# An attention and GEGLU kernel on one core: batch 0 in a new order, and gate matmuls placed around the last turn of each batch

## The chip, the core and the metric

The kernel runs on one core of a Trainium2 chip. The core has a matrix engine (PE, with its own queue of weight loads, PEld), a vector engine (DVE), a scalar engine (ACT) and GpSimd (POOL). SyncE (SP) and POOL also issue DMAs. Each engine works through its own instructions in program order, and they wait for each other through semaphores. Matmuls write into PSUM, of which this kernel uses all eight banks.

The metric is the device time of one execution in microseconds, as the median of several runs. One further execution was profiled. All times of single instructions are from that one.

## What is computed

There are 8 batches of 8 heads with 576 tokens of 64 elements, and 16 "beacon" keys and values in front of each head's own. After a causal softmax attention, the heads are put side by side to 4608 rows of 512, and a GEGLU block follows:

```python
k_all = np.concatenate([beacon_k, k], axis=2)
v_all = np.concatenate([beacon_v, v], axis=2)
scores = scale * np.matmul(q, k_all.transpose(0, 1, 3, 2))
scores = np.where(causal, -1000000000.0, scores)      # beacon columns are never masked
a = softmax(scores)
x = np.matmul(a, v_all)           # -> 4608 x 512
g, val = x @ w_gate, x @ w_val    # 512 x 1536 each
out = (gelu(g) * val) @ w_out     # 1536 x 512
```

Inputs and output are float32 in HBM. The loads convert to bfloat16 on the way.

## The kernel before, in words

Nearly every instruction is held in the order in which the program writes it (`keep`). So the order of the calls in the main loop is the order on each engine. The names that matter:

- A batch has four **pairs** of heads (`m` = 0 to 3). `scores(b, m, c)` (L205) does one of four chunks of transposed scores into a `psum_s` buffer and then an exponential on ACT into `expT`. Chunks 0 and 2 are called `ab(m)`, chunks 1 and 3 `cd(m)`. `masks` (L226) sets the masked triangle of `expT` to zero: on POOL (L239) for every batch but 0, on DVE (L236) for batch 0. `attend` (L254) is 30 small matmuls of `expT` with the values and a column of ones, `normalize` (L278) divides by the sum on DVE into `y_sb`; both together are `av(m)`. `turn(b, m)` (L294) transposes `y_sb` on PE and copies it on DVE into `xT_sb`, the input of the GEGLU block.
- `gate_val(ci, fi)` (L305) does one of 12 slices of the hidden layer for a chunk of 512 rows: 4 matmuls with the gate weights and 4 with the value weights (one for each `kk`, the four blocks of 128 of the input, which are the four pairs), into one `psum_s` buffer `gv_ps`. Then a GELU on ACT into `ge_sb`, and a product on DVE (L325) into `hT_sb`. The product is the last reader of `gv_ps`.
- `out_mms(ci, u0, u1)` (L330) does steps of the last matmul. A chunk has 48 steps, in four tiles of 12. After each 12th step DVE copies the tile out (L349) and SP stores it. The first tile of a chunk sits in `psum_t`, the others in `psum_o`. In the main loop `o(n)` means n steps of the chunk of the batch before.
- PSUM: `psum_s` has two buffers of two banks (scores, `gv_ps`, and one `attend` of batch 0), `psum_x` one of two banks (`attend`, and the PE transposes `t_ps`), `psum_t` and `psum_o` one bank each.
- Queries and keys of batches 0 and 1 are loaded by `load_qk6` and transposed on PE (`transpose_pe`, L162, 24 small transposes and one for the beacon keys, then two DVE copies into `qkT`). From batch 2 on they are loaded by `load_qk` into `q_sb` and `k_sb` and transposed by DMAs issued on SP (`transpose_dma`, L192).
- All loads are issued on POOL, in one queue with POOL's masks. Each issue from the ninth on waits until the DMA eight issues earlier has landed.

After the loads are issued, batch 0 does its four pairs with nothing to put between them but five `warm` matmuls (L187) after two of them; then 12 slices of `gate_val`, of which slices 6 to 9 are each followed by a `transpose_pe` of batch 1. From slice 0 on, the loads of batch 2 are queued on POOL. Batches 1 to 7 then have an attention part, in which the `o` steps fill the gaps, and a gate part of 12 slices. The first slice (`kk_late`) does its `kk` = 3 matmuls last, since those need the last turn. A last chunk of 512 rows is left over at the end.

The attention part of batches 1 to 7, in the order of PE before the change:

```
o5 ab0 o7 cd0 o5
ab1 av0 o3 cd1 o4 turn0
ab2 av1 o3 cd2 o5 turn1
ab3 av2 o4 cd3 o6 turn2
av3 o6 turn3  gate_val 0 .. 11
```

Of the kernel before, what the change touches and what calls it, by code (L numbers as in the profile page):

```python
# [7 lines left out]
P = 128  # L8
B, H, S, NB, D = 8, 8, 576, 16, 64
SK = S + NB  # L10
# [43 lines left out]
def kernel(  # L54
# [26 lines left out]

    ident = const.tile([P, P], BF16, name="ident", tag="ident")
    nc.vector.memset(ident, 0.0)
    wg_sb = const.tile([P, K_CHUNKS, D_FF], BF16, name="wg_sb", tag="wg_sb")
    wv_sb = const.tile([P, K_CHUNKS, D_FF], BF16, name="wv_sb", tag="wv_sb")
    wo_sb = const.tile([P, F_TILES, D_MODEL], BF16, name="wo_sb", tag="wo_sb")
# [22 lines left out]
    def dma(out_ap, in_ap):  # L109
        keep(nc.gpsimd.dma_start(out=out_ap, in_=in_ap))  # L110

    qk6 = {}

    def load_qk6(b, h0, h1):
        if b not in qk6:
            qk6[b] = (
                hpool.tile([P, 2, H, 6 * D], BF16, name="qk6", tag="hT_sb"),
                npool.tile([NB, H, D], BF16, name="kb", tag="kb"),
            )
        for w, src in enumerate((q, k)):  # L120
            dma(
                qk6[b][0][0:96, w, h0:h1, :],
                src[b, h0:h1, :, :].rearrange("h (p r) d -> p h (r d)", r=6),
            )

    def load_kb(b):
        dma(qk6[b][1], beacon_k[b].rearrange("h t d -> t h d"))

    def load_keys(src, beacon, dst, b):
        dma(dst[0:NB, 0, :, :], beacon[b].rearrange("h t d -> t h d"))  # L130
# [13 lines left out]
    def load_v(b):  # L144
        load_keys(v, beacon_v, v_ring[b % NRING][:, :, :, 0:D], b)

    def load_gate_val(i):
        fs = slice(i * 512, (i + 1) * 512)
        for w, dst in ((moe_w_gate, wg_sb), (moe_w_val, wv_sb)):
            keep(nc.gpsimd.dma_start(out=dst[:, :, fs], in_=w[:, fs].rearrange("(kk p) f -> p kk f", p=P)))  # L150

# [7 lines left out]
        keep(nc.scalar.activation(out_ap, in_ap, func, **kw))  # L159


    def transpose_pe(b, m, pool, tag):  # L162
        t_ps = pool.tile([P, 2, 1024], BF16, name="t_ps", tag=tag)
        qk, kb = qk6[b]

        def tr(out_ap, in_ap):
            n = in_ap.shape[0]
            keep(nc.tensor.transpose(out_ap, in_ap, ident[0:n, 0:n]))  # L168

        for w in range(2):  # L170
            for r in range(6):
                for hi in range(2):
                    tr(
                        t_ps[64 * hi : 64 * hi + 64, w, r * 96 : (r + 1) * 96],
                        qk[0:96, w, 2 * m + hi, r * D : (r + 1) * D],
                    )
        tr(t_ps[:, 1, S:SK], kb[:, 2 * m : 2 * m + 2, :])
        keep(
            nc.vector.tensor_copy(  # L179
                qkT[:, m, :, NB:SK].rearrange("p w (t r) -> p w t r", r=6),  # L180
                t_ps[:, 0:2, 0:S].rearrange("p w (r t) -> p w t r", r=6),
            )
        )
        keep(nc.vector.tensor_copy(qkT[:, m, 1, 0:NB], t_ps[:, 1, S:SK]))


    def warm(b, m, n):  # L187
        w_ps = psum_o.tile([P, D_MODEL], FP32, name="w_ps", tag="o")
        for _ in range(n):
            mm(w_ps, ident, qkT[:, m, 1, 0:512], True, True)  # L190

    def transpose_dma(b):  # L192
        q_sb, k_sb = q_ring[b % NRING], k_ring[b % NRING]
# [29 lines left out]
        if b:  # L223
            masks(b, m, c)

    def masks(b, m, c):  # L226
        expT = exp_of[b * NPAIR + m]
        for t, s_lo, _, _ in CHUNKS[c]:
            if s_lo != S_LO[t]:
                continue  # L230
            n = DIAG[t]
            d = expT[0 : KROWS[t], :, EXP_OFF[t] : EXP_OFF[t] + n]
            if b == 0:
                w = tri[0 : KROWS[t], NB : NB + n] if t == 0 else tri[0 : KROWS[t], 0:n]
                w = w.rearrange("p (o n) -> p o n", o=1).to_broadcast([KROWS[t], 2, n])
                keep(nc.vector.tensor_tensor(out=d, in0=d, in1=w, op=ALU.min))  # L236
            else:
                keep(
                    nc.gpsimd.affine_select(  # L239
                        out=d,  # L240
                        in_=d,
                        pattern=[[0, 2], [1, n]],
                        compare_op=ALU.is_ge,
                        fill=0.0,
                        base=NB if t == 0 else 0,
                        channel_multiplier=-1,
                    )
                )
# [42 lines left out]
                )  # L291
            )

    def turn(b, m):  # L294
        y_sb = y_of.pop(b * NPAIR + m).rearrange("p (j e) d -> p j (e d)", e=2)
        y_ps = psum_t.tile([P, 1024], BF16, name="y_ps", tag="t")
        for j in (4, 3, 2, 1, 0):
            n = P if j else S_LO[1]
            keep(nc.tensor.transpose(y_ps[:, Q_LO[j] : Q_LO[j] + n], y_sb[0:n, j, :], ident[0:n, 0:n]))  # L299
        keep(nc.vector.tensor_copy(xT_sb[:, m, b * S : (b + 1) * S], y_ps[:, 0:S]))  # L300


    h_of, o_of = {}, {}

    def gate_val(ci, fi, kk_late=False):  # L305
        if fi == 0:
            h_of[ci] = hpool.tile([P, F_TILES, CH], BF16, name="hT_sb", tag="hT_sb")
        n0 = ci * CH
        gv_ps = psum_s.tile([P, 2, CH], FP32, name="gv_ps", tag="s")
        order = [(w, kk) for w in range(2) for kk in range(K_CHUNKS)]  # L310
        if kk_late:
            order.sort(key=lambda t: t[1] == K_CHUNKS - 1)
        for w, kk in order:
            mm(
                gv_ps[:, w, :],
                (wg_sb, wv_sb)[w][:, kk, fi * P : (fi + 1) * P],
                xT_sb[:, kk, n0 : n0 + CH],
                kk == 0,
                kk == K_CHUNKS - 1,
                skip_group_check=True,  # L320
            )
        ge_sb = fpool.tile([P, CH], BF16, name="ge_sb", tag="ge_sb")
        act(ge_sb, gv_ps[:, 0, :], ACT.Gelu)
        keep(
            nc.vector.tensor_tensor(  # L325
                out=h_of[ci][:, fi, :], in0=gv_ps[:, 1, :], in1=ge_sb, op=ALU.mult
            )
        )

    def out_mms(ci, u0, u1, wide=lambda ti: False):  # L330
        for u in range(u0, u1):
# [22 lines left out]
    def by_diagonal(tile_, op, fill):  # L354
# [3 lines left out]
            )  # L358
        )

    load_qk6(0, 0, 2)
    by_diagonal(ident, ALU.not_equal, 1.0)
    load_kb(0)
    load_qk6(0, 2, 4)
    load_qk6(0, 4, H)
    by_diagonal(tri, ALU.is_ge, 0.0)
    load_v(0)
    for i in range(3):
        load_gate_val(i)
    load_qk6(1, 0, H)  # L370
    load_kb(1)
    load_out_w()
    load_v(1)
    transpose_pe(0, 0, psum_s, "s")
    for b in range(B):
        u = [0]

        def o(n):
            if b:
                out_mms(b - 1, u[0], u[0] + n, lambda ti: ti == 0)  # L380
                u[0] += n

        def ab(m):
            for c in AB:
                scores(b, m, c)

        def cd(m):
            for c in CD:
                scores(b, m, c)

        def av(m, wide=False):
            attend(b, m, wide)
            normalize(b, m)

        keep(nc.scalar.preload_act_table_set(SET_EXP))  # L395
        if b == 0:
            for m in range(NPAIR):
                ab(m)
                if m == NPAIR - 1:
                    for mm_ in (0, 1, 2):  # L400
                        for c in AB + CD:
                            if mm_ == 2 or (mm_ == 1 and c in CD):
                                masks(0, mm_, c)
                    av(0)
                    for c in AB:
                        masks(0, m, c)
                else:
                    transpose_pe(0, m + 1, psum_x, "x")
                    if m == 2:
                        for mm_, cs in ((0, AB + CD), (1, AB)):  # L410
                            for c in cs:
                                masks(0, mm_, c)
                cd(m)
                if 1 <= m < NPAIR - 1:
                    warm(b, m, 5)
            for c in CD:
                masks(0, NPAIR - 1, c)
            av(1)
            av(2, wide=True)
            turn(b, 0)  # L420
            turn(b, 1)
            av(3)
            turn(b, 2)
            turn(b, 3)
        else:
            o(5)
            ab(0)
            o(7)
            cd(0)
            o(5)  # L430
            for m in range(1, NPAIR):
                ab(m)
                av(m - 1)
                o((3, 3, 4)[m - 1])
                cd(m)
                o((4, 5, 6)[m - 1])
                turn(b, m - 1)
            av(3)
            o(6)
            turn(b, 3)  # L440
        keep(nc.scalar.preload_act_table_set(SET_GELU))
        for fi in range(F_TILES):
            gate_val(b, fi, kk_late=fi == 0)
            if b == 0 and 6 <= fi < 10:
                transpose_pe(1, fi - 6, psum_x, "x")
            if fi == 0:
                if b + 2 < B:
                    load_qk(b + 2)
# [37 lines left out]
```

## Time and profile before

| what | us |
|---|---|
| median of 4 runs (397.33 to 398.18) | 397.81 |
| the profiled execution | 397.34 |
| its span, first to last instruction | 395.6 |
| start to the first gate matmul of batch 0 (31.38) | 31.4 |
| gate part of batch 0, with the transposes of batch 1, to the first `o` step of batch 1 (55.98) | 24.6 |
| one later batch, from its first `o` step to that of the next one | 42.0 |
| of which attention with `o` steps | 21.3 |
| of which gate part | 20.7 |
| from the end of batch 7's gate part to the end | about 45 |

The span is shorter than the time of its execution by 1.7 us. Columns of the timeline are: start, duration, engine, line, operation, output and input with their shapes, how many instructions were merged into the row, and in brackets how long the engine stood idle before it and what ended that wait. Matmuls overlap at their ends, so a row's duration is longer than the step to the next row; steps between starts are what the engine takes.

### The profile page before, as it was taken

The page shows a single profiled execution, that of the slowest core. Times are in us where ns is not written, and L with a number is a line of the kernel's source. Part 1 is how long each engine was busy: PE and PEld are TensorE (multiplying, and loading weights), DVE is VectorE, ACT ScalarE, POOL GpSimd, SP SyncE. Part 2 cuts the span into 40 slices and gives each one's busy share as a digit, 9 for nine tenths or more (in the row PEclk, how much of TensorE's full clock was granted, in tenths as well). Part 3 has the DMA queues.
Part 4 walks back from the last instruction along what each step waited for, and adds up shares of the span by engine and source line. Part 5 has one row for each costly group of instructions (what it writes and reads, how often), then busy time and mean ns, then how long its engine had stood idle before and what let it go on. Part 6 is the DMA issues. An engine that isn't in the chain of part 4 may idle for free.

```text
span 395.6 us, 7386 instructions
## 1 busy us (share of the span) xinstructions
PE 371.3 (94%) x3010; PEld 183.0 (46%) x3010; DVE 167.2 (42%) x345; ACT 188.1 (48%) x252; POOL 155.6 (39%) x277
## 2 busy tenths in 40 slices
PE   3868999999999999999999999999999999999996
PEld 1454445544554445543544455444544455444442
DVE  1484554543354434433444345433444344332332
ACT  2852248433862378236833584338623782332210
POOL 8723494780368224941486047703300240000000
PEclk9999999999999999999999999999999999999999
DMA  7999996699029951998099916991142011000012
GB/s 95 177 206 204 179 135 90 65 155 139 35 56 150 134 65 46 136 151 83 29 116 141 101 55 67 151 135 36 55 104 44 30 41 41 2 0 28 29 51 106
DMA packets 139153, 36.23 MB, mean 92 GB/s; under 512 B 126832, under 2 KB 134512, under 8 KB 139120
## 3 DMA queue, kind: packets, MB, share of 16 engines
q0 software_dynamic: 103984, 19.14, 63.6%
q1 hardware_dynamic: 35136, 16.62, 21.4%
q8 instruction: 23, 0.38, 0.4%
q14 instruction: 10, 0.08, 0.1%
HBM read 38.27 MB, written 9.44 MB: 121 GB/s over the span
## 4 chain that ended last, share of the span: by engine, by line
PE 75%; DVE 9%; ACT 6%; DMA 5%; issue 3%; POOL 2%; POOLq 0%; DVEq 0%
PE gv_ps L156 41%; PE o_ps L156 16%; PE x_ps L156 7%; PE s_ps L156 6%; DVE y_sb L289 4%; ACT expT L159 3%; PE y_ps L299 2%; DMA qkT<-q_sb 2%; DMA v_sb<-in_beacon_v_dram 2%; ACT L395 1%; PE t_ps L168 1%; ACT ge_sb L159 1%; DVE r_sb L287 1%; DVE o_sb L349 1%; DVE qkT L179 1%
## 5 line engine op out<-in xcount | busy, mean ns | idle before, releaser
L159 ACT ACTIVATE ge_sb<-gv_ps 128x512 bf16<-128x512 f32 x108 | 64.5, 597 | 165.2 <-PE gv_ps L156 165.2
L325 DVE TENSOR_TENSOR hT_sb<-gv_ps,ge_sb 128x512 bf16<-128x512 f32 x108 | 74.7, 692 | 124.9 <-ACT ge_sb L159 123.0
L159 ACT ACTIVATE expT<-s_ps 128x1024 bf16<-128x1024 f32 (+3 forms) x128 | 103.1, 861 | 27.0 <-PE s_ps L156 24.9
L156 PE MATMUL gv_ps<-xT_sb,wg_sb 128*128 128x512 bf16 x432 | 112.2, 379 | 0.0
L156 PE MATMUL gv_ps<-xT_sb,wv_sb 128*128 128x512 bf16 x432 | 112.2, 379 | 0.0
L156 PE MATMUL o_ps<-wo_sb,hT_sb 128*128 128x512 bf16 x432 | 106.9, 379 | 5.3 <-DVE o_sb L349 5.3
L239 POOL TENSOR_SCALAR_AFFINE_SELECT expT<-expT 128x256 bf16<-128x256 bf16 (+2 forms) x140 | 51.5, 387 | 137.1 <-ACT expT L159 137.1
L156 PEld LDWEIGHTS <-wv_sb 128*128 128x128 bf16 x432 | 42.3, 98 | 51.0
L156 PEld LDWEIGHTS <-wg_sb 128*128 128x128 bf16 x432 | 41.6, 98 | 48.2
L156 PEld LDWEIGHTS <-hT_sb 128*128 128x128 bf16 x432 | 38.0, 98 | 45.8 <-issue 6.6
L156 PE MATMUL s_ps<-qkT 64*128 64x336 bf16 (+5 forms) x384 | 38.0, 291 | 4.8 <-ACT expT L159 1.9
L110 POOL DMA_DIRECT2D v_sb<-in_v_dram x40 | 33.8, 862 | 18.9 <-DMA wv_sb<-in_moe_w_val_dram 3.6
L349 DVE COPY o_sb<-o_ps 128x512 f32<-128x512 f32 x36 | 24.8, 688 | 27.1 <-PE o_ps L156 27.1
L156 PEld LDWEIGHTS <-expT 128*128 128x128 bf16 (+1 forms) x960 | 31.1, 97 | 8.2 <-POOL expT L239 7.0
L156 PE MATMUL x_ps<-v_sb,expT 128*128 128x65 bf16 x930 | 33.6, 193 | 0.6 <-DVE y_sb L289 0.6
L289 DVE TENSOR_TENSOR y_sb<-x_ps,r_sb 128x384 bf16<-128x384 f32 (+1 forms) x62 | 30.4, 491 | 2.1
L156 PEld LDWEIGHTS <-qkT 64*128 64x128 bf16 x384 | 14.3, 95 | 30.8 <-issue 22.9
L110 POOL DMA_DIRECT2D q_sb<-in_q_dram x30 | 25.3, 855 | 5.9 <-DMA wo_sb<-in_moe_w_out_dram 5.9
L287 DVE RECIPROCAL r_sb<-x_ps 128x6 f32<-128x6 f32 (+1 forms) x62 | 11.4, 184 | 35.8 <-PE x_ps L156 35.8
L110 POOL DMA_DIRECT2D k_sb<-in_k_dram x30 | 25.4, 890 | 0.0
L300 DVE COPY xT_sb<-y_ps 128x576 bf16<-128x576 bf16 x32 | 14.5, 453 | 22.1 <-PE y_ps L299 22.1
L299 PE MATMUL y_ps<-ident,y_sb 128*128 128x128 bf16 (+1 forms) x160 | 14.1, 218 | 4.5 <-DVE xT_sb L300 3.4
(33 smaller groups left out, 91.4 us busy)
## 6 DMA issues: line engine op xcount, KB each, us to landing
out_dram<-o_sb SPq DMA_DIRECT2D x36, 256.0 KB, 2.0
v_sb<-in_v_dram POOLq DMA_DIRECT2D x24, 128.0 KB, 10.6
q_sb<-in_q_dram POOLq DMA_DIRECT2D x24, 128.0 KB, 4.4
k_sb<-in_k_dram POOLq DMA_DIRECT2D x18, 128.0 KB, 7.9
wg_sb<-in_moe_w_gate_dram POOLq DMA_DIRECT2D x3, 512.0 KB, 10.4
wv_sb<-in_moe_w_val_dram POOLq DMA_DIRECT2D x3, 512.0 KB, 12.2
wo_sb<-in_moe_w_out_dram POOLq DMA_DIRECT2D x1, 1536.0 KB, 24.0
v_sb<-in_v_dram POOLq DMA_DIRECT2D x8, 112.0 KB, 9.1
```

The source lines that it names most:

```text
L110: keep(nc.gpsimd.dma_start(out=out_ap, in_=in_ap))
L156: keep(nc.tensor.matmul(out_ap, lhsT, rhs, start=start, stop=stop, **kw))
L159: keep(nc.scalar.activation(out_ap, in_ap, func, **kw))
L168: keep(nc.tensor.transpose(out_ap, in_ap, ident[0:n, 0:n]))
L179: nc.vector.tensor_copy(qkT[:, m, :, NB:SK].rearrange("p w (t r) -> p w t r", r=6), t_ps[:, 0:2, 0:S].rearrange("p w (r t) -> p w t r", r=6),)
L239: nc.gpsimd.affine_select(out=d, in_=d, pattern=[[0, 2], [1, n]], compare_op=ALU.is_ge, fill=0.0, base=NB if t == 0 else 0, channel_multip ...
L287: keep(nc.vector.reciprocal(r, x[:, :, D:DV]))
L289: nc.vector.tensor_tensor(out=y_sb[:, j0 : j0 + n, :], in0=x[:, :, 0:D], in1=r.to_broadcast([P, n, D]), op=ALU.mult)
L299: keep(nc.tensor.transpose(y_ps[:, Q_LO[j] : Q_LO[j] + n], y_sb[0:n, j, :], ident[0:n, 0:n]))
L300: keep(nc.vector.tensor_copy(xT_sb[:, m, b * S : (b + 1) * S], y_ps[:, 0:S]))
L325: nc.vector.tensor_tensor(out=h_of[ci][:, fi, :], in0=gv_ps[:, 1, :], in1=ge_sb, op=ALU.mult)
L349: keep(nc.vector.tensor_copy(o_sb[:, ti, :], o_ps))
```

## The change

It has these parts:

1. **Start.** The beacon keys of batch 0 come through SP as float32 and are converted by a DVE copy. Eight matmuls on a zeroed tile (`idle`) run on PE ahead of any data. Queries and keys of batch 0 are loaded two heads at a time, keys first, in eight DMAs (before: two pairs of two heads and one of four). The gate and value weights come in slices of 256, 256, 512 and 512 columns (before: three of 512).
2. **Batch 0.** Pairs 0 and 2 are transposed in halves, keys and queries apart, the query half of pair 0 copied by ACT. Masks, `av`, turns and the copies after turns (now `put`, apart from `turn`) get a new order by hand. The masks of pair 3 go to POOL, between the load issues of batch 1, which move behind pair 3's scores in the program. The copy after turn 2 goes to ACT.
3. **First two gate slices of batch 0.** Their matmuls are split by `kk` and placed around turns 2 and 3. The second slice uses `psum_x`.
4. **Batches 1 to 7.** The `o` steps get another spread, `av` moves behind `o` steps, and six of the eight matmuls of slices 0 and 1 are placed before and after the last turn. Both slices use `psum_s`. Then come the two `kk` = 3 matmuls of slice 0, those of slice 1, and the GELU and product of each (`gv_close`).
5. **Transposes of batch 1** follow slices 8 to 11 instead of 6 to 9.

The order of batches 1 to 7 on PE after it:

```
o6 ab0 o8 cd0 o6
ab1 o4 av0 cd1 o4 turn0
ab2 o4 av1 cd2 o4 turn1
ab3 o4 av2 cd3 o4 turn2
o4 av3 gv0(kk 0-2) turn3 gv1(kk 0-2) gv0(kk 3) gv1(kk 3)  gate_val 2 .. 11
```

The core of the diff:

```diff
+    idle = const.tile([P, 512], BF16, name="idle", tag="idle")
+    nc.vector.memset(idle, 0.0)
...
-        for w, src in enumerate((q, k)):
+        for w, src in ((1, k), (0, q)):
             dma(
...
-    def load_gate_val(i):
-        fs = slice(i * 512, (i + 1) * 512)
+    def load_gate_val(f0, f1):
+        fs = slice(f0 * P, f1 * P)
...
+    def transpose_half(b, m, w, by_act=False):
+        pool, tag = ((psum_o, "o"), (psum_t, "t"))[w]
+        t_ps = pool.tile([P, 1024], BF16, name="t_ps", tag=tag)
+        tr_part(b, m, w, t_ps)
+        out_ap = qkT[:, m, w, NB:SK].rearrange("p (t r) -> p t r", r=6)
+        in_ap = t_ps[:, 0:S].rearrange("p (r t) -> p t r", r=6)
+        if by_act:
+            act(out_ap, in_ap, ACT.Copy)
+        else:
+            keep(nc.vector.tensor_copy(out_ap, in_ap))
+        if w:
+            keep(nc.vector.tensor_copy(qkT[:, m, 1, 0:NB], t_ps[:, S:SK]))
+
+    def warm(n, pool, tag):
+        w_ps = pool.tile([P, D_MODEL], FP32, name="w_ps", tag=tag)
+        for j in range(n):
+            mm(w_ps, idle[:, 128 * (j % 4) : 128 * (j % 4) + 128], idle, True, True)
...
+    def gv_mms(ci, fi, *kks, pool=None, tag="s"):
+        if (ci, fi) not in gv_of:
+            gv_of[ci, fi] = (pool or psum_s).tile([P, 2, CH], FP32, name="gv_ps", tag=tag)
+        gv_ps = gv_of[ci, fi]
+        n0 = ci * CH
+        for w in range(2):
+            for kk in kks:
+                mm(
+                    gv_ps[:, w, :],
+                    (wg_sb, wv_sb)[w][:, kk, fi * P : (fi + 1) * P],
+                    xT_sb[:, kk, n0 : n0 + CH],
...
+    kb_sb = opool.tile([NB, H, D], FP32, name="kb_sb", tag="o_sb")
+    keep(nc.sync.dma_start(out=kb_sb, in_=beacon_k[0].rearrange("h t d -> t h d")))
     load_qk6(0, 0, 2)
...
+    load_gate_val(0, 2)
+    load_gate_val(2, 4)
+    load_gate_val(4, 8)
+    load_gate_val(8, 12)
...
+    keep(nc.scalar.preload_act_table_set(SET_EXP))
+    warm(8, psum_x, "x")
+    keep(nc.vector.tensor_copy(qk6[0][1], kb_sb))
+    transpose_half(0, 0, 1)
+    transpose_half(0, 0, 0, by_act=True)
+    c(0, *AB)
+    transpose_pe(0, 1)
+    mk(0, AB)
+    c(0, *CD)
+    transpose_half(0, 2, 1)
+    transpose_half(0, 2, 0)
+    mk(0, CD)
+    c(1, *AB)
+    transpose_pe(0, 3)
+    c(1, 1)
+    warm(3, psum_t, "t")
+    mk(1, AB)
+    c(1, 3)
+    warm(1, psum_o, "o")
+    mk(1, CD)
+    c(2, *AB)
+    av(0, 0)
+    c(2, 1)
+    warm(2, psum_o, "o")
+    c(2, 3)
+    mk(2, AB)
+    c(3, *AB)
+    load_qk6(1, 0, 4)
+    mk(3, AB, by_dve=False)
+    mk(2, CD)
+    turn(0, 0)
+    av(0, 1)
+    put(0, 0)
+    c(3, *CD)
+    load_qk6(1, 4, H)
+    mk(3, CD, by_dve=False)
+    load_kb(1)
+    load_out_w()
+    load_v(1)
+    turn(0, 1, psum_o, "o")
+    put(0, 1)
+    av(0, 2)
+    av(0, 3, wide=True)
+    gv_mms(0, 0, 0, 1)
+    turn(0, 2)
+    put(0, 2, by_act=True)
+    keep(nc.scalar.preload_act_table_set(SET_GELU))
+    gv_mms(0, 1, 0, 1, pool=psum_x, tag="x")
+    turn(0, 3, psum_o, "o")
+    put(0, 3)
+    for kk in (2, 3):
+        for fi in (0, 1):
+            gv_mms(0, fi, kk)
     for b in range(B):
...
+            o(4)
+            av(b, 3)
+            keep(nc.scalar.preload_act_table_set(SET_GELU))
+            gv_mms(b, 0, 0, 1, 2)
+            turn(b, 3)
+            put(b, 3)
+            gv_mms(b, 1, 0, 1, 2)
+            gv_mms(b, 0, 3)
+            gv_mms(b, 1, 3)
         for fi in range(F_TILES):
-            gate_val(b, fi, kk_late=fi == 0)
-            if b == 0 and 6 <= fi < 10:
-                transpose_pe(1, fi - 6, psum_x, "x")
+            if fi < 2:
+                gv_close(b, fi)
+            else:
+                gate_val(b, fi)
+            if b == 0 and fi >= 8:
+                transpose_pe(1, fi - 8)
             if fi == 0:
                 if b + 2 < B:
                     load_qk(b + 2)
```

## The prediction

> **What bounds the kernel now.** I read the page first, then the windows of one later batch, the timeline of that batch, the waits of PE, and POOL's own timeline up to batch 1.
>
> ```profile
> PE 371.3 (94%) x3010; PEld 183.0 (46%) x3010; DVE 167.2 (42%) x345; ACT 188.1 (48%) x252; POOL 155.6 (39%) x277
> ```
>
> PE is busy 94% of the span, so what counts is where PE stands still. In the windows (start and end, length, then busy us of PE, PEld, DVE, ACT, POOL) the gate part has no gap, and the attention part of the same batch lacks 1.05 us:
>
> ```profile
> 140.20:161.49 21.29, 20.24 (x237) 10.77 (x236) 9.53 (x24) 16.06 (x19) 10.59 (x24) 1.00 0.29 52
> 161.49:182.20 20.71, 20.71 (x98) 9.40 (x96) 8.11 (x13) 6.57 (x11) 10.38 (x14) 1.00 1.88 151
> ```
>
> The timeline of this batch gives every price that I need for batches 1 to 7:
>
> ```profile
> 140.02 1.24 PE L156 MATMUL o_ps<-wo_sb,hT_sb 128*128 128x512 bf16 x5
> 140.22 0.60 ACT L159 ACTIVATE ge_sb<-gv_ps 128x512 bf16<-128x512 f32 x1 [1.13 <-PE gv_ps L156]
> 140.85 0.69 DVE L325 TENSOR_TENSOR hT_sb<-gv_ps,ge_sb 128x512 bf16<-128x512 f32 x1 [1.04 <-ACT ge_sb L159]
> ...
> 156.22 0.68 DVE L349 COPY o_sb<-o_ps 128x512 f32<-128x512 f32 x1
> 156.96 1.46 PE L156 MATMUL o_ps<-wo_sb,hT_sb 128*128 128x512 bf16 x6 [0.76 <-DVE o_sb L349]
> ...
> 159.44 1.46 PE L156 MATMUL o_ps<-wo_sb,hT_sb 128*128 128x512 bf16 x6
> 159.65 0.20 DVE L287 RECIPROCAL r_sb<-x_ps 128x6 f32<-128x6 f32 x1 [0.47 <-PE x_ps L156]
> ...
> 160.56 0.42 DVE L289 TENSOR_TENSOR y_sb<-x_ps,r_sb 128x256 bf16<-128x256 f32 x1
> ...
> 161.05 0.45 PE L299 MATMUL y_ps<-ident,y_sb 128*128 128x128 bf16 x5
> ```
>
> Two chains are to be seen. A gate slice ends on PE at 140.02; GELU starts 0.20 later, the product ends at 141.54, so its buffer is back 1.52 us after the slice, 1.58 with the 0.06 that PE took after the DVE copy (156.90 to 156.96). And `av` ends at 159.44, its `y_sb` at 160.98, and the turn starts at 161.05: 1.61 us. Six `o` steps cover 1.30 of these; PE waits 0.31.
>
> Last, POOL (the idle time in brackets is the wait for the output weights to land):
>
> ```profile
> 46.47 3.32 POOL L110 DMA_DIRECT2D q_sb<-in_q_dram  x4 [5.89 <-DMA wo_sb<-in_moe_w_out_dram]
> 49.75 0.57 POOL L110 DMA_DIRECT2D k_sb<-in_beacon_k_dram  x1
> 50.28 4.23 POOL L110 DMA_DIRECT2D k_sb<-in_k_dram  x5
> 54.43 0.60 POOL L110 DMA_DIRECT2D v_sb<-in_beacon_v_dram  x1
> 54.96 4.26 POOL L110 DMA_DIRECT2D v_sb<-in_v_dram  x5
> 59.19 0.44 POOL L239 TENSOR_SCALAR_AFFINE_SELECT expT<-expT 128x224 bf16<-128x224 bf16 x1
> ```
>
> POOL issues batch 2's loads without a pause from 46.47 to 59.2, and only then the first mask of batch 1, which `av0` of batch 1 needs. Before, that mask's scores are ready just then. POOL is idle nowhere here, so a batch 1 that starts sooner finds its masks no sooner.
>
> **Batches 2 to 7.** PE's total work is the same: 48 `o` steps, four pairs, 96 gate matmuls. Only waits change.
>
> Gone: (a) `ab0` starts one `o` step later (0.216), past the product of the last gate slice, which held its second chunk (PE took 0.70 from 141.20 to 141.90, against 0.52 from 149.27): 0.18. (b) `cd0` comes two steps later, after the exponentials that held its second chunk (143.52 to 144.24 is 0.72, against 0.42 from 147.61): 0.30. (c) The tile borders now fall at the end of an `o` group (24, 36 and 48 steps), with `av`, `cd` or a turn and `ab` behind them, so the copy of 0.69 is covered: 0.76. Sum 1.24.
>
> New: (d) turns 0 to 2 come after `cd` (0.10 gap and 0.42) and four steps (0.87), 1.39 behind `av`, and need 1.61: 0.22 each, taken as 0.21, sum 0.63. Bounds: 0 if `cd` is as slow as in (b), 0.3 as now. Turn 3 has six gate matmuls in front in place of six `o` steps: 0.31 as before. (e) The `kk` = 3 matmuls of slices 0 and 1 follow each other. Slice 2 needs the buffer of slice 0, 1.58 after slice 0's last matmul, and only slice 1's two matmuls (0.43) stand between: 1.15. Before, all eight of slice 1 (1.73) stood there, so the wait was 0. Sum 1.78. (f) Nothing else: the copy after turn 3 (0.46, starting 0.2 behind the turn) is covered by six matmuls (1.30); `av3` starts 2.65 after `cd3` does (0.42, 0.87, a turn with its wait 0.49, 0.87), and the masks end 2.52 after it (155.73 to 158.25), 0.1 before they are needed; without that cover they would cost the difference.
>
> Net 0.54 a batch, for six batches +3.2. In one boundary (batch 5 to 6) PE waited 0.5 for a DMA transpose. The stores that stand ahead of the transposes on SP come 1.5 to 2 us sooner (tile 4 is done before `av3`), so I take that off: -0.5; kept, it is 0.
>
> **Batch 0.** Its new length is a chain. The last values land as before at about 17.3 (issued near 10.6, 6.7 to landing), or 0.7 later, since two more issues of 0.65 to 0.75 stand ahead and one of 0.56 goes. Behind the first `av` come the six exponentials of pairs 2 and 3: 1.38 + 1.86 + 1.38 = 4.6, so about 23.2. Three masks on POOL 1.05, the rest of `av3` 0.5, normalize 1.6, turn 0.45, copy 0.66, four matmuls 0.86: slices 0 and 1 end near 28.5, where they ended at 34.84 (6.3 sooner). DVE, converting the beacon keys and clearing `idle`, and ACT, copying twice, do it before these points; if not, 0.7 each. The halved weight slices have landed by then: the first 512 columns of both landed at 22.2, and the same bytes come in the same order.
>
> The other ten slices take 17.3, four transposes 3.2, their waits 0.7 as now: batch 1 starts near 49.7 instead of 55.98. Its `av0` comes 6.96 later (six steps 1.30, `ab0` with its gap 0.62, eight steps 1.73, `cd0` 0.52, 1.30, `ab1` 0.62, four steps 0.87), at 56.7.
>
> **Where this gain goes.** POOL is not there. Up to the landing of the output weights the same bytes move, and from 17 to 44 us the DMA moves 202 to 209 GB/s whatever waits for them; the queue stays full, because the loads of batch 1 now wait on POOL for landings at 19 to 23 while 2 MB of weights are queued. So the landing stays at 46.5 (bounds 46.0 and 47.0), sixteen issues follow, and the masks start at 59.2. Five take 0.44 + 0.35 + 1.05, to 61.0; fifteen small matmuls of `av0` come after the last (0.5): `av0` ends at 61.56. Before it ended at 62.83. Seven more `o` steps lie behind PE by then (1.51), and the waits after it are 0.63 + 1.15 - 0.76 = 1.02 more. At slice 2 batch 1 is 1.27 + 1.51 - 1.02 = 1.76 sooner. Of the 6.3 of batch 0 most is lost in this one wait of 2.9.
>
> **Sum.** 395.6 - 1.76 + 3.24 - 0.5 = 396.6 of span, +1.0. The profiled run (397.34, 1.7 of it outside the span) is 0.5 under the median, which I carry along: 397.81 + 1.0 = 398.8.
>
> **A rule that speaks against the change.** From the trace: five `warm` matmuls took 2.00 us at 14.89 and 1.25 at 19.36, although the granted clock reads 1.00 in every window; PE's longest wait after that, 1.92 before 27.94, left the next turn at 0.45, as later. The Trainium skill, TensorE: Matmul & The Clock Gate, section on the HAM clock gate, says that PE falls to half its clock after an idle window of about 3.4 us and needs one busy window to return. The wait of 2.9 in batch 1 is just below it: by the trace it costs nothing, by the rule nothing too unless batch 0 ends 0.5 sooner than I reckon, and then, as an estimate from that page, 3.4 us at half clock, 1.7 us.
>
> **Rivals.**
> - *The clock drops in the wait of batch 1.* For: a wait 1.5 times the longest that the trace shows as harmless. Against: `o` steps right before it. Price from the trace: PE worked without a break from 12.05 to 16.8 before the faster steps came, 4.7 us at half speed, 2.4 lost: 401.2. Chance 0.14.
> - *POOL doesn't hold batch 1, faster than before.* If the output weights land 3 us sooner, since batch 0's loads are finer and one small load leaves POOL, `av0` runs at 56.7 and ends at 57.6, 4.0 sooner: 394.8. A landing at 45.5 takes the 1.0 away, one at 44.7 makes the kernel faster by 0.2%. Against: the steady 206 GB/s. Chance 0.10.
> - *Slice 2 doesn't wait for the product* (e). If its buffer came back with the GELU (0.72 less), seven batches save 5.0: 393.8. Against: `ab0` after the last slice was held until the product had ended. Chance 0.10.
> - *Batch 0 gains nothing*, because a landing or the slow first matmuls hold it: then POOL is not waited for, and each of seven batches costs its 0.54: 397.81 + 3.8 - 0.5 = 401.1. For: eight landings are now waited for one by one. Chance 0.08.
>
> **How the numbers follow.** My forecast has 0.58. Its own range follows from (d) 0 to 0.3 a turn (-4.4 to +1.9 over seven batches, the ends unlikely in all of them), POOL's landing ±0.5 and the DMA transpose 0 to 0.5: 397.0 to 400.2. A measurement of this kernel tells 0.2%, 0.8 us, from no change. Within the forecast, 0.30 lies above 398.6, 0.24 within and 0.04 below 397.0. With the rivals (0.22 slower, 0.20 faster; of the first some 0.02 stays within), slower has 0.50, the same 0.26, faster 0.24. The range goes up to 401.6, to take in the slower rivals with the 0.4 of a landing, and down to 396.6, where the two faster rivals (0.20) are left out.
>
> **What would show it.** Right: in batches 1 to 7 a PE wait of about 1.15 at the third gate slice, ended by the product on DVE; three waits of 0.2 before turns; no wait for `o_sb`; a later batch of 42.5 instead of 42.0. In batch 1 a PE wait of about 3 before `av0`, ended by POOL, with POOL issuing loads until 59. Batch 0's first two slices near 28.5. Wrong: masks of batch 1 on POOL before 57, or slice 2 following slice 1 without a gap.

## The result, and the profile after

| what | before | after |
|---|---|---|
| median, us (range, executions) | 397.68 (396.3 to 401.08, 56) | 399.84 (398.32 to 401.11, 37) |
| ratio after / before, 95% interval | | 1.0045 [1.0034, 1.0056] |
| the profiled execution, its span | 397.34, 395.6 | 398.48, 396.8 |
| first `o` step of batch 1 | 55.98 | 51.13 |
| first `o` step of batch 2 | 97.99 | 95.45 |
| one later batch | 42.03 | 42.60 |
| first `o` step of the last chunk | 352.07 | 352.74 |

The change makes the kernel slower by 0.45%: batch 0 hands over 4.85 us sooner, of which 2.54 are left at batch 2 and nothing at the end. The engine table and the granted clock of the page (busy us, share of the span, instructions; the clock in tenths for 40 slices):

```profile
PE 377.4 (95%) x3014; PEld 183.1 (46%) x3014; DVE 167.0 (42%) x342; ACT 189.1 (48%) x254; POOL 159.8 (40%) x287
PEclk9599999999999999999999999999999999999999
```

PE is busy for 6.1 us more (377.4 against 371.3) with four matmuls more: a higher busy share is no sign of a faster kernel. The clock falls once, in the second slice, which is in batch 0 and is looked at below.

Windows of one later batch after the change (start and end, length, then busy us of PE, PEld, DVE, ACT, POOL, then clock and DMA), cut at the last turn's end:

```profile
95.45:117.32 21.87, 21.54 (x241) 11.06 (x240) 9.81 (x24) 16.11 (x19) 10.08 (x24) 1.00 0.18 43
117.32:138.05 20.73, 19.75 (x96) 8.97 (x95) 7.98 (x12) 6.46 (x11) 10.80 (x14) 1.00 1.89 149
```

The gap has changed sides. Before, the attention part lacked 1.05 and the gate part nothing. Now the attention part lacks 0.33 and the gate part 0.98. (The 0.33 is less than its gaps, since the modelled ends of matmuls reach into each of them.) The waits of PE name that gap (us in total, times, longest):

```profile
PE gv_ps L161 <- DVE hT_sb L357: 6.9, 7, 1.0
PE y_ps L169 <- DVE y_sb L309: 0.9, 1, 0.9
PE x_ps L161 <- DVE o_sb L385: 0.7, 1, 0.7
PE x_ps L161 <- POOL expT L259: 0.2, 1, 0.2
```

Seven times, once in each of batches 1 to 7, gate matmuls wait 0.98 for the product. No `o_ps` waits for an output copy any more. The timeline of batch 2 shows both places:

```profile
102.46 1.08 PE L161 MATMUL x_ps<-v_sb,expT 128*128 128x65 bf16 x30
103.47 0.47 PE L161 MATMUL s_ps<-qkT 64*128 64x64 bf16 x8
103.87 1.04 PE L161 MATMUL o_ps<-wo_sb,hT_sb 128*128 128x512 bf16 x4
104.97 0.45 PE L169 MATMUL y_ps<-ident,y_sb 128*128 128x128 bf16 x5
...
119.42 0.38 PE L161 MATMUL gv_ps<-xT_sb,wv_sb 128*128 128x512 bf16 x1
120.78 1.02 PE L161 MATMUL gv_ps<-xT_sb,wg_sb 128*128 128x512 bf16 x4 [0.98 <-DVE hT_sb L357]
```

Four `o` steps take 0.87 of PE, so PE is through at 104.74, and the turn starts 0.23 later. Slice 1's last matmul is done at 119.64 (0.216 after its start), and slice 2 starts 1.14 later. The bracket shows only 0.98, since it counts from the modelled end of that matmul (119.42 + 0.38 = 119.80).

POOL up to batch 1 after the change, and below it PE around the first `attend` of batch 1:

```profile
45.78 3.31 POOL L112 DMA_DIRECT2D q_sb<-in_q_dram  x4 [6.19 <-DMA wo_sb<-in_moe_w_out_dram]
54.25 4.26 POOL L112 DMA_DIRECT2D v_sb<-in_v_dram  x5
58.42 2.51 POOL L259 TENSOR_SCALAR_AFFINE_SELECT expT<-expT 128x224 bf16<-128x224 bf16 x7
```

```profile
57.20 1.04 PE L161 MATMUL o_ps<-wo_sb,hT_sb 128*128 128x512 bf16 x4
58.98 1.10 PE L161 MATMUL x_ps<-v_sb,expT 128*128 128x65 bf16 x15 [0.74 <-DVE o_sb L385]
60.31 0.63 PE L161 MATMUL x_ps<-v_sb,expT 128*128 128x65 bf16 x15 [0.24 <-POOL expT L259]
```

PE is through with the four `o` steps at 58.07 and starts `attend` at 58.98. The wait is named after the copy of `o_sb`, but the name is a trap: `attend` writes no buffer that this copy reads. The weight load of the same `attend`, on PE's queue for those, has the true one:

```profile
58.97 0.14 PEld L161 LDWEIGHTS <-expT 128*128 128x128 bf16 x3 [1.23 <-POOL expT L259]
```

It needs POOL's first masks, which start at 58.42. POOL is 0.7 sooner than before (45.78 against 46.47), and batch 1 comes to it 4.85 sooner. That is the place where batch 0's gain stops.

One number is not in this profile: the spans of the two profiled executions differ by 1.2, the medians by 2.2. Over the 37 executions the span has its median at 398.1, and only eight are under 397.4. The profiled one, 396.8, is one of the shortest. What the typical execution has on top is settled by experiments.

### The profile page after: what moved, and what is told of

Read it like the earlier page. It is cut to its first block, busy times and chain, and to the rows that moved or that the text cites. A ratio compares the mean times of both kernels' runs of the same rounds, so it can differ in the third digit from the quotient of the medians.

```text
span 396.8 us, 7407 instructions
## 1 busy us (share of the span) xinstructions
PE 377.4 (95%) x3014; PEld 183.1 (46%) x3014; DVE 167.0 (42%) x342; ACT 189.1 (48%) x254; POOL 159.8 (40%) x287
## 4 chain that ended last, share of the span: by engine, by line
PE 71%; DVE 11%; DMA 9%; POOL 6%; issue 2%; ACT 1%; POOLq 0%
PE gv_ps L161 39%; PE o_ps L161 18%; DVE y_sb L309 7%; PE x_ps L161 6%; DMA wo_sb<-in_moe_w_out_dram 5%; PE s_ps L161 4%; PE y_ps L169 3%; DMA wv_sb<-in_moe_w_val_dram 3%; DVE r_sb L307 2%; POOL v_sb L112 2%; DVE hT_sb L357 1%; POOL qk L112 1%; DMA k_sb<-in_k_dram 1%; ACT ge_sb L164 1%; POOL q_sb L112 1%
## 5 line engine op out<-in xcount | busy, mean ns | idle before, releaser
L164 ACT ACTIVATE ge_sb<-gv_ps 128x512 bf16<-128x512 f32 x108 | 63.6, 597 | 154.2 <-PE gv_ps L161 152.2
L161 PE MATMUL gv_ps<-xT_sb,wg_sb 128*128 128x512 bf16 x432 | 113.8, 379 | 6.9 <-DVE hT_sb L357 6.9
L161 PE MATMUL gv_ps<-xT_sb,wv_sb 128*128 128x512 bf16 x432 | 113.8, 379 | 0.0
L259 POOL TENSOR_SCALAR_AFFINE_SELECT expT<-expT 128x256 bf16<-128x256 bf16 (+2 forms) x145 | 52.8, 388 | 135.8 <-ACT expT L164 135.8
L161 PEld LDWEIGHTS <-expT 128*128 128x128 bf16 (+1 forms) x960 | 33.5, 98 | 9.0 <-POOL expT L259 1.8
L161 PE MATMUL s_ps<-qkT 64*128 64x336 bf16 (+5 forms) x384 | 36.3, 291 | 1.1 <-ACT qkT L164 0.7
L161 PEld LDWEIGHTS <-qkT 64*128 64x128 bf16 x384 | 13.0, 95 | 17.0 <-issue 11.3
L169 PEld LDWEIGHTS <-y_sb 128*128 128x128 bf16 (+1 forms) x160 | 9.2, 97 | 17.8 <-DVE y_sb L309 17.3
```

Of the source, the lines that this page charges most:

```text
L161: keep(nc.tensor.matmul(out_ap, lhsT, rhs, start=start, stop=stop, **kw))
L259: nc.gpsimd.affine_select(out=d, in_=d, pattern=[[0, 2], [1, n]], compare_op=ALU.is_ge, fill=0.0, base=NB if t == 0 else 0, channel_multip ...
```

## The experiments

All times are medians, ratios are against the kernel before on the same chip.

### Part by part: batches 1 to 7 alone, batch 0 alone

The kernel before with only the new order of batches 1 to 7 (`o` steps, `av` behind them, two slices split, as in the change's second list of the main loop), batch 0 untouched:

```diff
-            o(5)
+            o(6)
             ab(0)
-            o(7)
+            o(8)
...
+            gv_mms(b, 0, 0, 1, 2)
             turn(b, 3)
+            gv_mms(b, 1, 0, 1, 2)
+            gv_mms(b, 0, 3)
+            gv_mms(b, 1, 3)
```

> The kernel before, with the new order of batches 1 to 7 alone. Theory: each batch takes 0.57 longer, seven times, less 0.2 for the DMA transpose that is no longer waited for: +3.8 us, 401.5, ratio 1.0095. Rival: the loss sits in batch 0 or in what it does to batch 1, and this one is within 0.8 us of the kernel before.

Measured: 401.71 (10 executions), ratio 1.0096 [1.0063, 1.0129], a later batch 42.59. The new order alone costs about 1%, as summed: 0.56 for each of the batches.

The changed kernel with the old order in batches 1 to 7, so batch 0 of the change alone:

```diff
-            o(6)
+            o(5)
             ab(0)
-            o(8)
+            o(7)
...
-            gv_mms(b, 1, 0, 1, 2)
             gv_mms(b, 0, 3)
-            gv_mms(b, 1, 3)
```

> The changed kernel's batch 0, with the order of batches 1 to 7 of the kernel before. Theory: batch 1 starts about 5 us sooner, but its av0 ends no sooner than POOL allows (60.8 instead of 62.8), so 2 us remain: 395.7, ratio 0.995. Rival: PE's wait for POOL is an effect of the new order only, and 4 to 5 us remain (0.988). Rival 2: batch 0 is where typical runs lose time against the profiled one; then it is no faster than the kernel before.

Measured: 397.32 (12 executions), ratio 0.9984 [0.9961, 1.0008], a later batch 42.03. This is a miss of 1.6 us: a batch 0 shorter by some 5 us brings nothing that can be told from none. The timeline of PE in this run:

```profile
59.35 2.34 PE L161 MATMUL x_ps<-v_sb,expT 128*128 128x65 bf16 x30 [3.16 <-POOL expT L259]
61.49 1.04 PE L161 MATMUL o_ps<-wo_sb,hT_sb 128*128 128x512 bf16 x2
```

and the windows of the same stretch, PE alone (length, PE busy, granted clock, DMA share, GB/s):

```profile
58.00:60.00 2.00, 0.65 (x8) 0.53 2.21 141
60.00:64.00 4.00, 3.61 (x37) 0.50 0.92 58
64.00:65.00 1.00, 1.00 (x3) 0.52 0.00 0
```

PE waits 3.16 for POOL's masks, and from about 58, still within that wait, the clock is at a half for more than 6 us: `attend`, once it runs, takes 2.14 from start to next start, where it takes 1.01 at full clock (102.46 to 103.47 above). Batch 2 starts near 98.26, no sooner than before (97.99). So there are two thieves at one place, POOL's queue and the clock.

### POOL's queue: the first masks of batch 1 on DVE

```diff
-            masks(b, m, c)
+            masks(b, m, c, b == 1 and m == 0)
```

> The changed kernel, with the five masks of pair 0 of batch 1 on DVE instead of POOL. Theory: av0 of batch 1 waits only because its masks stand behind POOL's load issues; it then ends near 59.0 instead of 60.8 in the span, and the kernel takes 1.8 us less than the changed one (398.0, ratio 1.001). Rival 1: another wait stands behind it (values not landed, DVE late), less than 0.5 us. Rival 2: the time over the profiled execution (median 399.8, profile 398.5) comes from this wait, which differs from run to run with the landing of the output weights; then the gain is about 3 us and the spread of the runs is smaller.

Measured: 395.65 (12 executions), ratio 0.9939 [0.9914, 0.9965]: 4.2 under the changed kernel, more than either theory gave it. PE, and then POOL, of this run:

```profile
56.84 1.04 PE L161 MATMUL o_ps<-wo_sb,hT_sb 128*128 128x512 bf16 x4
57.71 1.08 PE L161 MATMUL x_ps<-v_sb,expT 128*128 128x65 bf16 x30
58.72 0.47 PE L161 MATMUL s_ps<-qkT 64*128 64x64 bf16 x8
```

```profile
54.13 4.26 POOL L112 DMA_DIRECT2D v_sb<-in_v_dram  x5
58.30 0.85 POOL L259 TENSOR_SCALAR_AFFINE_SELECT expT<-expT 128x224 bf16<-128x224 bf16 x2
```

`attend` follows the `o` steps without a gap, while POOL issues loads to 58.30 as it did. The profiled spans differ by 2.2 (394.6 against 396.8), which is the wait for POOL: batch 3 starts 2.16 sooner (135.89 against 138.05). The rest of the 4.2 lies in the typical executions, whose median span falls from 398.1 to 393.95. With the wait went something that the profile of the changed kernel does not show. (Some 0.65 of the 4.2 is only that this profiled execution is itself longer than its kernel's median span: 394.6 against 393.95.)

### The clock: is it the rest?

In the changed kernel, eight idle matmuls on the zeroed tile are put into the wait, so that PE does not stand still:

```diff
             o(4)
+            if b == 1:
+                warm(8, psum_x, "x")
             av(b, 0)
```

> The changed kernel with eight matmuls on the zeroed tile (1.73 us at full clock) ahead of av0 of batch 1, in PE's wait for POOL. They add work that fits into the wait. Theory: the wait's second cost is the clock; with PE kept at work it doesn't drop, and the median comes down to about 398.4, with the spread of e2 (1.7) instead of 2.8. Rival: the drop is not what lifts the median; then the time is 399.8 or, if the matmuls don't fit in, up to 1 more.

Measured: 399.0 (8 executions), ratio 1.0040 [1.0026, 1.0054], against 398.4 expected. The time is 0.6 off, and the ratio alone does not tell this kernel from the changed one (1.0045). In two of the eight executions 2.8 us lie outside the span instead of 1.7 to 2.0. The spans are clear: 396.9 to 397.8, median 397.15, where the changed kernel has 396.6 to 399.4, median 398.1. Seven of these eight are under 397.4, against eight of its 37. Timeline of PE:

```profile
56.98 1.89 PE L161 MATMUL w_ps<-idle 128*128 128x512 bf16 x8
59.51 1.10 PE L161 MATMUL x_ps<-v_sb,expT 128*128 128x65 bf16 x15 [0.64 <-POOL expT L259]
```

`attend` starts later than in the profile after (59.51 against 58.98), so no wait was saved, and still the long spans are gone. The clock reads 1.00 from 58 to 66.

The changed kernel without the eight idle matmuls at the start (`w_ps` before any data) was meant to price these, and its profile happens to be of a typical execution:

```diff
     keep(nc.scalar.preload_act_table_set(SET_EXP))
-    warm(8, psum_x, "x")
     keep(nc.vector.tensor_copy(qk6[0][1], kb_sb))
```

> The changed kernel without the same eight matmuls. Theory: POOL frees batch 1 whenever batch 0 ends, so a longer batch 0 is not felt: 399 to 400, as the changed kernel (399.84), or up to 0.8 less, because a shorter wait before av0 of batch 1 lets the clock drop less often. Rival: batch 0's length counts, and what e10 loses against e9 is lost here too.

Measured: 399.79 (12 executions), ratio 1.0041 [1.0016, 1.0066], as with them. Its timeline at the wait:

```profile
56.75 1.04 PE L161 MATMUL o_ps<-wo_sb,hT_sb 128*128 128x512 bf16 x4
59.15 1.10 PE L161 MATMUL x_ps<-v_sb,expT 128*128 128x65 bf16 x15 [1.36 <-POOL expT L259]
60.48 0.63 PE L161 MATMUL x_ps<-v_sb,expT 128*128 128x65 bf16 x15 [0.24 <-POOL expT L259]
```

Windows of PE there, first this kernel, then the profiled execution of the changed kernel (columns as above):

```profile
58.00:60.00 2.00, 0.73 (x13) 1.00 2.12 135
60.00:62.00 2.00, 1.76 (x31) 0.83 1.90 211
62.00:64.00 2.00, 1.78 (x10) 0.50 0.19 28
64.00:66.00 2.00, 2.00 (x20) 0.81 0.04 8
```

```profile
58.00:60.00 2.00, 1.14 (x17) 1.00 2.00 138
60.00:62.00 2.00, 1.76 (x30) 1.00 1.99 207
62.00:64.00 2.00, 1.94 (x15) 1.00 0.21 47
64.00:66.00 2.00, 2.00 (x43) 1.00 0.00 0
```

The next scores and the third `attend` of batch 1, in the same order:

```profile
63.85 1.00 PE L161 MATMUL s_ps<-qkT 64*128 64x512 bf16 x4
...
69.93 1.08 PE L161 MATMUL x_ps<-v_sb,expT 128*128 128x65 bf16 x30
```

```profile
62.75 0.58 PE L161 MATMUL s_ps<-qkT 64*128 64x512 bf16 x4
...
68.42 1.08 PE L161 MATMUL x_ps<-v_sb,expT 128*128 128x65 bf16 x30
```

The two are alike up to 61. Here the gap before `attend` is 1.53 (57.62 to 59.15), there 0.91. Some 2 us after `attend` has begun, the clock falls to 0.50 here, and the same four score matmuls take 1.00 instead of 0.58. The first `attend` starts 0.17 later than there, the third 1.51 later, so the drop costs 1.3 in this execution. (The counts of matmuls, 20 against 43, are no measure: other matmuls stand in that window.) Over its 12 executions the mean granted clock sorts the spans: 0.999 or 1.000 goes with 396.8, 396.8 and 396.9, and 0.995 or 0.996 with 397.3 to 399.1 (nine executions, median 398.2). With what the longer gap adds, the drop costs about 1.4, and it comes three times in four. The changed kernel's own executions fit: with a mean clock of 0.999 the spans are 396.8 and 397.0, with 0.993 to 0.996 they are 398.3 to 399.2 (five executions). With 0.983 (five) they are 398.8 to 399.4. Most of the others read 0.987, which a drop in batch 0 gives alone, as in the profile; a shorter drop there with one in the wait would read the same, and their spans go from 396.6 to 398.8.

### The gate slot: slice 2 without the wait

Slice 1 gets the free `psum_x` buffer, so that slice 2 doesn't need slice 0's:

```diff
-            gv_mms(b, 1, 0, 1, 2)
+            gv_mms(b, 1, 0, 1, 2, pool=psum_x, tag="x")
```

> The changed kernel, with the second gate slice of batches 1 to 7 in psum_x, as batch 0 has it. In the changed kernel's trace PE waits 7 times 0.98 us for the product on DVE before the third slice. Theory: this wait is the loss of batches 1 to 7, so 6.9 us go: 393 us (ratio to the kernel before 0.988), a later batch of 41.6 us instead of 42.6. Rival: the wait only moves, to the buffer of slice 3 or to DVE, and the time stays within 1 us of 399.8 (1.003 to 1.006).

Measured: 391.93 (6 executions), ratio 0.9842 [0.9805, 0.9878], a later batch 41.45, so 1.15 less. Slice 2 follows at once in the timeline:

```profile
161.61 0.38 PE L161 MATMUL gv_ps<-xT_sb,wv_sb 128*128 128x512 bf16 x1
161.82 1.03 PE L161 MATMUL gv_ps<-xT_sb,wg_sb 128*128 128x512 bf16 x4
```

Seven times 1.15 is 8.05, and the median fell by 7.9. This one line turns the loss into a gain of 1.6%. The wait of batch 1 is still there, and longer (2.02 from 57.49 to 59.51), and its clock reads 0.92, 0.50 and 0.73 in the two-us windows from 60 to 66.

### Putting them together

Both edits (slot and masks):

> The changed kernel with both repairs: the second gate slice in psum_x (e1) and the masks of pair 0 of batch 1 on DVE (e2). Theory: the two losses are in different places and add: 399.84 - 7.9 - 4.2 = 387.7, ratio 0.975. Rival: with the steps of e1 earlier in batch 1 another wait (values, POOL's masks of pair 1) takes part of it, 389 or more.

Measured: 387.66 (4 executions), ratio 0.9748 [0.9729, 0.9766]. They add up: 399.84 - 7.9 - 4.2 = 387.7.

On top of it, another spread of the `o` steps, so that five of them cover each of turns 0 to 2:

```diff
             cd(1)
-            o(4)
+            o(5)
             turn(b, 0)
...
             ab(2)
-            o(4)
+            o(2)
             av(b, 1)
             cd(2)
-            o(4)
+            o(5)
...
```

> e7 with the o steps of batches 1 to 7 spread 6, 8, 6, 4, 5, 2, 5, 3, 5, 4 instead of 6, 8, 6 and seven times 4, so that each of turns 0 to 2 has one step (0.216) more ahead of it and the tile borders stay at ends of groups. Theory: PE stands 0.21 before each of the three turns, which goes: 7 x 0.63 = 4.4 less than e7, 383.3. Rival: scores or masks are late where an ab has only two or three steps behind it, and the wait moves there: less than 2 us of gain.

Measured: 385.46 (5 executions), ratio 0.9694 [0.9672, 0.9716], a later batch 41.07: half of the gain that was expected (2.2 of 4.4). Timeline of PE:

```profile
184.18 0.60 PE L161 MATMUL o_ps<-wo_sb,hT_sb 128*128 128x512 bf16 x2
184.62 1.07 PE L161 MATMUL x_ps<-v_sb,expT 128*128 128x65 bf16 x30
185.62 0.70 PE L161 MATMUL s_ps<-qkT 64*128 64x64 bf16 x8
186.26 1.25 PE L161 MATMUL o_ps<-wo_sb,hT_sb 128*128 128x512 bf16 x5
187.35 0.44 PE L169 MATMUL y_ps<-ident,y_sb 128*128 128x128 bf16 x5
```

The turn now follows its five steps (1.08) almost at once. But the two steps taken from in front of `attend` were cover, too: the eight score matmuls of `cd2` take 0.64 to the next start, in place of 0.40 (103.47 to 103.87 above), because their buffers wait for the exponentials of `ab2`, and ACT works without a break from 184.15 to 187.43. This was no row of the waits view; it shows only in the steps between starts.

Then two matmuls of slice 1 in front of turn 3, for which slices 1 and 2 swap their buffers:

```diff
             gv_mms(b, 0, 0, 1, 2)
+            gv_mms(b, 1, 0)
             turn(b, 3)
             put(b, 3)
-            gv_mms(b, 1, 0, 1, 2, pool=psum_x, tag="x")
+            gv_mms(b, 1, 1, 2)
...
+            elif b and fi == 2:
+                gv_mms(b, fi, *range(K_CHUNKS), pool=psum_x, tag="x")
+                gv_close(b, fi)
```

> e8 with two of slice 1's matmuls (0.43) moved ahead of turn 3 in batches 1 to 7; for that slice 1 takes psum_s again and slice 2 psum_x. In e8 PE still stands about 0.31 before turn 3 (the matmul ahead of it ends 1.30 after av3, the turn starts 1.61 after it). Theory: 7 x 0.31 = 2.2 less than e8: 383.3, a later batch of 40.75 instead of 41.07. Rival: the copy after turn 3 has only four matmuls (0.86) over it then, 0.46 and 0.2 of latency; if that doesn't fit, less than 1 us is gained.

Measured: 383.1 (6 executions), ratio 0.9630 [0.9596, 0.9663], a later batch 40.74. Windows of one later batch, in one piece:

```profile
131.27:172.01 40.74, 40.05 (x328) 20.32 (x332) 17.77 (x36) 22.57 (x30) 20.93 (x37) 1.00 1.13 104
```

Of a later batch 0.69 is left in which PE is not busy; in the changed kernel it was 1.31. This version beats the kernel before by 14.5 us and the changed one by 16.7.

The same without the idle matmuls at the start:

> e9 without the eight matmuls on the zeroed tile at the start. Here nothing behind batch 0 swallows its length, so it shows what they are worth. Theory: without them the first transposes and scores of batch 0 run at half speed and the first exponential comes about 0.5 us later, but the end of batch 0 hangs on the values' landing and on ACT: 0.5 us slower than e9 or less. Rival: the clock stays low through batch 0, 1 to 3 us slower.

Measured: 383.09 (6 executions), ratio 0.9625 [0.9589, 0.966]. In both pairs, this one and the changed kernel with and without them, these eight matmuls are worth nothing that can be measured. The windows of PE in batch 0 of the changed kernel show part of the reason:

```profile
6.00:12.00 6.00, 4.05 (x64) 0.67 1.39 156
12.00:18.00 6.00, 6.00 (x52) 0.50 1.93 176
```

The first scores behind them are quick (0.59 for four at 6.69), but then the clock falls, and the next four, at 11.81, take 1.00, as long as before. And in four of the eight profiled kernels that have these matmuls (gate slot, masks on DVE, batch 0 alone, the new spread) the first scores are not quick either. The gate slot's:

```profile
7.04 1.00 PE L161 MATMUL s_ps<-qkT 64*128 64x512 bf16 x4 [0.75 <-ACT qkT L164]
```

The granted clock reads 1.00 there all the same, so at the start it does not tell slow matmuls from fast ones.

## Why the prediction was right, and what it had wrong

The forecast of a slight slowdown held, at 399.84 against 398.8, but one term that it had put among the rivals belongs into the sum.

**Waits of batches 1 to 7: right in each term.** (a) to (c): the wait for `o_sb` is gone and those of the first scores with it. (d) turns 0 to 2 wait 0.23 in the trace, against 0.21 to 0.22. (e) slice 2 waits 1.14, against 1.15; removing it alone gave 1.15 a batch. Net +0.57 a batch, against +0.54, and shown apart by the run with only this part (42.59). For six batches this is 3.4.

**The DMA transpose: mis-sized.** Taken off were 0.5. The batch in which that wait stood was longer than its neighbours by 0.18 only (42.21 against 42.03), so 0.18 is all that could go. The other 0.3 of that wait must have stood in the place of waits that come without it, which was only inferred.

**Batch 0: 1.5 too short, at no price.** Slices 0 and 1 were to end near 28.5; they end at 29.99. The eight exponentials of pairs 2 and 3 run without a break from 17.36 for 6.82 us, to 24.18, where the sum had their end at 23.2. At the end of the masks (25.44 for 24.25) the lag is 1.2, and at the end of pair 3's `y_sb` (27.85 for 26.35) 1.5, since DVE normalizes pair 2 first, from 25.27 to 26.60. From there it goes as summed. Batch 1 starts at 51.13 instead of 49.7. This execution is late: in the seven other traces with this batch 0 and its idle matmuls batch 1 starts at 49.91 to 50.77. Here the clock is at a half from about 8.0 to 18.3; in the trace with 49.91 it is back at about 15.7. None of this changes the end through PE's work, because batch 1 waits for POOL. But the later batch 1 starts, the shorter is that wait (0.91 at 51.13, 1.53 at 50.68, 2.02 at 50.54), which may be why this execution kept its clock; no run shows that.

**POOL's queue: right in kind, mis-sized by 0.7.** The output weights land at 45.78, just outside the bounds of 46.0 to 47.0, so `attend` of batch 1 ends at 60.8 instead of 61.56. Batch 2 is 2.54 sooner, against 1.76. That the loads in POOL's queue hold the first masks is shown by the run with these masks on DVE: with the loads where they were, the wait is gone.

**Sum for the profiled execution.** -2.54 + 6 x 0.57 - 0.18 = +0.70; the last chunk starts 0.67 later (352.74 against 352.07). The last output copy starts 0.66 later (392.65 against 391.99). The end of the last store adds 0.5: 396.8 - 392.65 is 4.15, against 3.61 before. 396.6 of span were forecast, 396.8 came. The 0.5 was in no step. That the two spans are so close is partly luck: the errors of -0.8 (batch 1), +0.2 (six batches), +0.3 (transpose) and +0.5 (store) nearly cancel.

**The clock in the wait of batch 1: the step that failed.** The forecast took it for a rival with a chance of 0.14 and a price of 2.4, because the longest wait of the profile before, 1.92, had left the clock alone, and took the wait of 2.9 that it expected for harmless. That premise came from one execution. Of 27 executions of the kernel before that ran beside the first four experiments, eight have a mean clock of 0.991 or 0.996 and spans of 397.2 to 399.7; the others have 0.999 or 1.000 and at most 396.6. So the clock falls in some executions of the kernel before, too; where, no trace shows. After the change a drop comes in most executions and costs about 1.4. That it exists in a typical execution is shown by the trace without idle matmuls at the start, and that keeping PE at work in the wait takes the long spans away by the run that does so. For the changed kernel as it is, no profile of an execution with the drop was taken; its spans (median 398.1, against 396.8 where it is absent) and their mean clocks fit it, and that part is inferred. The profiled spans differ by 1.2, the medians by 2.2; the 1.0 between them is most of what the forecast of +1.0 lacked. The 0.4 that are left of the 1.4 are owed to the kernel before, whose median span of 396 is that much longer than its profiled 395.6.

A rule that the prediction weighed does not fit these traces. The Trainium skill, TensorE: Matmul & The Clock Gate, section on the HAM clock gate, has the clock fall after an idle window of about 3.4 us. Here gaps of 1.53 and 2.02 before a thinly filled 2 us were enough, while a gap of 0.91 was not. The measurement decides: a full window without work is not needed here. A clock that falls after a stretch with too little work fits these rows, but that is a reading and not shown: in the profile before, a wait of 1.92 with further waits behind it left the clock at 1.00.

**The other rivals.** *POOL doesn't hold batch 1*: no, POOL does. *Slice 2 doesn't wait for the product*: it does, 0.98 in each of seven batches. *Batch 0 gains nothing*: false for batch 0 itself, which is 4.85 shorter, but true for the kernel: with batch 0 of the change alone, the ratio is 0.9984 [0.9961, 1.0008], not because of a landing in batch 0 but by what batch 1 finds.

What stays open: what decides in a single execution whether the clock falls (four traces with waits of 0.91 to 3.16, and three in twelve executions of one and the same kernel without the drop, give no threshold), and why the last store takes 0.5 longer.

## What to carry to other kernels

When two accumulation groups are interleaved and closed one right after the other, count how much work then stands before the next user of their buffers: here 0.43 us of matmuls had to cover a chain of 1.58 us through ACT and DVE, and a third, idle buffer was worth 1.15 us a batch. An engine that is far from busy can still set the time if its queue mixes DMA issues with work that others need, so a stage made shorter in front of it only waits longer, and with PE the wait costs a second time when the clock falls. A profile of one execution can be the lucky one: compare its span with those of all executions before you take it for the kernel.

## What the runs showed of the hardware

- The granted clock fell to 0.50 about 2 us after `attend` began to run thinly, not in the wait itself, and stayed down for about 3.4 us, as summed from the windows: behind a gap of 1.53 (0.83, 0.50, 0.81 in the windows from 60 to 66) and one of 2.02 (0.92, 0.50, 0.73). In a named wait of 3.16, which ends at 59.35, it was already at 0.53 in 58 to 60, and it was low for more than 6 us.
- Matmuls on zeros ahead of the data raised the speed of the next few matmuls in four of eight traces (0.59 instead of 1.00 for four of 512 columns). In the profile after, the clock so gained was lost again from about 8.0 to 18.3, and two pairs of kernels show no gain (383.1 and 383.09; 399.84 and 399.79).
- The mean granted clock of an execution sorts its spans only where the drop lies on the path. In batch 0, whose end is swallowed by the wait for POOL, half a clock for ten microseconds (the 0.987 of the profiled execution after) goes with the shortest spans as well. Nor does a mean of 1.00 say that batch 0 ran fast: where the first scores take 1.00, the clock reads 1.00 too.
